# A condition around a loop that may have no turns, with its semaphores reset in stages

## The chip, the cores and the metric

The kernel runs on one core of a Trainium2 chip. Times are device microseconds of that core. The engines are named as the profile names them: PE (matrix multiply; PEld its weight loads), DVE (vector), ACT (scalar), POOL (GpSimd) and SP (SyncE, which here issues DMAs). Each engine has a sequencer of its own (PEq, DVEq and so on in the rows), which runs branches, register moves, semaphore waits and drains; the profile does not count these as busy.

## The reference

Three parts run one after the other on 1152 tokens: attention with rotary positions, a dense feed-forward layer, and a layer of eight experts, of which each token goes to one. Cut to what matters here:

```python
def _moe2_ref(x, w_gate, w1, w2, capacity):
    expert_idx = np.argmax(x @ w_gate, axis=1)
    ...
    for i in range(N):                      # tokens in order, up to capacity for each expert
        e = expert_idx[i]
        if counts[e] < capacity:
            disp[e, counts[e]] = x[i]
            ...
    h = np.maximum(np.einsum('ecd,edf->ecf', disp, w1), 0.0)
    y = np.einsum('ecf,efd->ecd', h, w2)
    ... # out[i] = gate_w[i] * y[expert_idx[i], pos[i]] for kept tokens
```

How many tokens an expert gets is known only at run time.

## The kernel before, in words

`whole` builds the attention (`Attention.run`, an order written out by hand) and then `Experts.run`. The last runs the dense layer in three column ranges (`first`), and between them sorts the tokens of each of the two batches by expert (`route`). Sorted tokens are cut into items: an item is up to 288 tokens of one expert. Four items always exist, of fixed widths (`STATIC`), and are written out in straight code: three calls of `second` and one of `few`. An input that spreads its tokens more evenly makes more items than four, up to 20. For these the kernel holds a loop, `tc.For_i(4, n, 1)` at line 1214, whose body gathers an item's rows, turns them, runs one expert and sends the result. `route` writes the number of items into the last place of the table `etab`, and line 1213 loads it into a register of every engine as `n`.

The last piece of straight work is `few`. Its last step is on POOL: `send` (line 1081), a DMA that scatters 96 rows to `out`. Behind it on POOL stand the load of `n`, the loop's entry, and the end of the program.

A layer under the kernel records the operations, orders them and puts in the semaphores. Each engine counts its work on a semaphore of its own; DMAs that SP issues count on eight semaphores (DMAHW0 to DMAHW7), and DMAs that POOL issues on eight others (DMASW0 to DMASW7). After the loop, the numbers on these semaphores must be the same whether or not it had a turn. So an engine that skips the loop adds to its semaphores what the loop would have added. For the POOL DMAs one instruction on POOL does it: INC_SWDGE_SEM in the profile, ISA in the listings below.

The built program of before has these blocks in this order behind the straight code: *skip* (taken when `n` is 4), *reset* (a barrier and the reset of all semaphores, before each further turn), *body*, *exit*, *end*. In *skip* POOL waits until all of its DMAs, the last `send` among them, have landed, and then adds. In *exit* each of the five engines passes a list of twelve waits on pairs of semaphores: all DMAs, all engines. In *end* SP waits for nothing more; every engine drains, meets the others in a barrier that POOL leads, POOL clears the semaphores, and there is a second barrier.

A drain is the instruction by which the program has an engine finish what it has in hand. The rows give the end block line 1244, the loop and its blocks line 1214.

Of the kernel before, what the change touches and what calls it, by code (L numbers as in the profile page):

```python
# [322 lines left out]
class Attention:  # L323
# [280 lines left out]
    def run(self, spare):  # L604
        for _, _, f, args in plan(len(spare)):
            self.pin((lambda: spare[args[0]]()) if f == "spare" else (lambda: getattr(self, f)(*args)))
# [57 lines left out]
class Experts:  # L664
# [527 lines left out]
    def run(self):  # L1192
        nc, tc = self.nc, self.tc
        sp = [mybir.EngineType.SP]
        found, x = {}, {}

        def turn(i):
            x[i] = self.turn(found[i][1], i)

        self.logits = [self.two.tile([TT, NT, E], F32, name=f"logits{b}", bufs=1) for b in range(B)]  # L1200
        for n, (k0, k1) in enumerate(zip(CUTS, CUTS[1:])):
            self.first(k0, k1, {0: (10, self.setup), len(CUTS) - 2: (0, lambda: turn(0))}.get(n))
            if n == 0:
                self.clear()
            for b in range(B):
                if k0 < (b + 1) * NT <= k1:
                    self.route(b, self.logits[b])
                    for k in range(2 * b, 2 * b + 2):
                        found[k] = self.gather(k, [b], *STATIC[k])
        for i in range(3):  # L1210
            self.second(found[i][0], x[i], self.expert(i, sp), ((4, 0, 4)[i], lambda: turn(i + 1)))
        self.few(found[3][0], x[3], self.expert(3, sp))
        n = nc.values_load(self.etab[0:1, ITEMS:ITEMS + 1], min_val=4, max_val=ITEMS)
        with tc.For_i(4, n, 1) as i:
            ent, rows = self.gather(i, [0, 1])
            self.cut = []
            self.second(ent, self.turn(rows, 0), self.expert(i, sp))
# [30 lines left out]
```

## Time and profile before

| | us |
|---|---|
| median of 3 runs | 460.74 (460.49 to 464.29) |
| the profiled execution, its own time | 461.19 |
| its span, from first to last instruction | 459.4 |
| the rest, around the span | 1.8 |

The span counts every instruction, those of the sequencers too. PE is busy for 436.6 us of it (95%), at a mean granted clock of 0.994. What lies in the last microseconds is not matrix work, and is read from the rows of the sequencers, line by line in narrow stretches.

### The profile page before, as it was taken

To read this page: it belongs to the slowest core of one execution; us is meant where nothing else is said; L and a number is where in the kernel's file an instruction comes from. 1 tells how busy PE (TensorE), PEld (TensorE's weight loads), DVE (VectorE), ACT (ScalarE), POOL (GpSimd) and SP (SyncE) were. 2 spreads that over 40 slices of the span, in tenths; PEclk is the share of its full clock that TensorE was granted. 3 is DMA by queue.
4 is the path that set the end of the run, shared out by engine and by line. 5 is a ranking of instruction groups with operands and counts; after the bars stand their busy time and mean duration, and the time that the engine had idled before them with its cause. 6 is when DMAs were issued, how large, how long until landed. Compare 5 with 4: busy or idle time off the path is not lost.

```text
span 459.4 us, 9065 instructions
## 1 busy us (share of the span) xinstructions
PE 436.6 (95%) x3380; PEld 373.4 (81%) x3380; DVE 309.7 (67%) x693; ACT 266.0 (58%) x558; POOL 123.9 (27%) x130
## 2 busy tenths in 40 slices
PE   7899999999988999999999999999999999999991
PEld 3556666666565878788999999999999999999980
DVE  5866866677968889997355344457846697765670
ACT  1788888888858252445453445475566455464560
POOL 1589877983210000000000000000526033701020
PEclk9999999999999999999999999999999999999997
DMA  8614421331315756550011600001175446874510
GB/s 279 235 71 145 144 72 75 144 122 30 139 53 177 257 165 245 216 188 1 0 36 34 224 0 1 0 27 46 6 271 182 145 139 186 247 260 157 185 51 16
DMA packets 20319, 57.11 MB, mean 124 GB/s; under 512 B 3749, under 2 KB 5957, under 8 KB 20272
## 3 DMA queue, kind: packets, MB, share of 16 engines
q1 hardware_dynamic: 17584, 52.09, 33.4%
q0 software_dynamic: 1728, 3.62, 2.6%
q10 hardware_dynamic: 960, 0.79, 0.5%
q8 instruction: 28, 0.46, 0.4%
q14 instruction: 19, 0.16, 0.1%
HBM read 49.91 MB, written 6.66 MB: 123 GB/s over the span
## 4 chain that ended last, share of the span: by engine, by line
PE 57%; issue 15%; DVE 10%; DMA 9%; POOL 4%; ACT 3%; SPq 0%; POOLq 0%; DVEq 0%; ACTq 0%
PE h L758 18%; PE y L784 17%; PE t L576 7%; PE s L461 6%; PE t L501 5%; DMA slots<-entry,r_at 2%; DMA raw<-in_w_in 2%; DVE pp L473 2%; POOL slots L959 2%; PE tr L849 2%; POOL out L1081 2%; DVE wf L659 2%; PE s L450 2%; DMA ent<-slots 1%; DVE m L658 1%
## 5 line engine op out<-in xcount | busy, mean ns | idle before, releaser
L758 PE MATMUL h<-xt,hl 128*128 128x288 f32 (+3 forms) x864 | 159.9, 324 | 3.5 <-ACT hl L744 1.4
L758 PEld LDWEIGHTS h<-xt,hl 128*128 128x128 f32 x864 | 135.2, 188 | 11.2 <-ACT hl L744 2.4
L784 PE MATMUL y<-gh,hl 128*128 128x288 f32 (+3 forms) x576 | 123.9, 322 | 0.4 <-ACT gh L794 0.4
L745 DVE TENSOR_TENSOR hl<-wf,hl 128x1024 fp32r<-128x1024 f32 x72 | 87.9, 1224 | 51.3 <-ACT hl L744 51.2
L744 ACT ACTIVATE hl<-wf 128x1024 fp32r<-128x1024 f32 x72 | 76.1, 1059 | 49.6 <-DVE wf L659 26.1
L784 PEld LDWEIGHTS y<-gh,hl 128*128 128x128 f32 x576 | 94.9, 188 | 4.3 <-ACT gh L794 0.8
L784 PE MATMUL y<-gl,hl 128*128 128x288 f32 (+3 forms) x288 | 77.0, 321 | 0.0
L959 POOL DMA_INDIRECT slots<-entry,r_at x12 | 15.0, 1254 | 208.0 <-ACT hl L744 184.3
L793 ACT ACTIVATE g<-h 128x480 f32<-128x480 f32 (+2 forms) x48 | 23.2, 491 | 63.1 <-PE h L758 54.3
L473 DVE TENSOR_SCALAR_CACHE_REDUCE pp<-s 128x576 f32<-128x576 f32 x64 | 45.8, 754 | 16.2 <-PE s L461 15.8
L485 ACT ACTIVATE pp<-pp,nm 128x576 f32<-128x576 f32 x64 | 49.3, 771 | 12.5 <-DVE pp L473 11.8
L784 PEld LDWEIGHTS y<-gl,hl 128*128 128x128 f32 x288 | 50.9, 188 | 1.8
L795 DVE TENSOR_TENSOR gl<-g,gh 128x480 fp32r<-128x480 f32 (+2 forms) x48 | 26.5, 555 | 27.5 <-ACT gh L794 27.2
L434 POOL TENSOR_TENSOR qk<-qk,turns 128x640 f32<-128x640 f32 (+1 forms) x28 | 41.5, 1507 | 9.5 <-DMA qk<-in_qk 9.5
L461 PE MATMUL s<-qk 64*128 64x288 f32 x256 | 40.8, 421 | 3.1 <-DVE pp L473 1.4
L382 ACT ACTIVATE pt<-t 128x512 f32<-128x512 f32 (+1 forms) x65 | 32.8, 538 | 10.4 <-PE t L501 10.3
L576 PE MATMUL t<-pt,vr 128*64 128x288 f32 x256 | 38.3, 419 | 0.1
L501 PEld LDWEIGHTS t<-ident,pp 64*128 64x128 f32 x576 | 23.7, 138 | 16.2 <-issue 4.2
L501 PE MATMUL t<-ident,pp 64*128 64x64 f32 x576 | 28.8, 230 | 2.6 <-ACT pt L382 0.9
L461 PEld LDWEIGHTS s<-qk 64*128 64x128 f32 x256 | 24.0, 188 | 8.3 <-DVE pp L473 2.6
L576 PEld LDWEIGHTS t<-pt,vr 128*64 128x64 f32 x256 | 15.5, 136 | 13.4 <-issue 3.8
L794 ACT ACTIVATE gh<-g 128x480 fp32r<-128x480 f32 (+2 forms) x48 | 24.8, 525 | 1.1
(173 smaller groups left out, 473.6 us busy)
## 6 DMA issues: line engine op xcount, KB each, us to landing
wf<-in_w SPq DMA_DIRECT2D x32, 512.0 KB, 4.5
qk<-in_qk SPq DMA_DIRECT2D x14, 640.0 KB, 5.5
raw<-in_w_in SPq DMA_DIRECT2D x16, 512.0 KB, 4.4
raw<-in_w_out SPq DMA_DIRECT2D x16, 512.0 KB, 3.8
vr<-in_v SPq DMA_DIRECT2D x8, 320.0 KB, 5.0
x<-row SPq DMA_DIRECT2D x12, 192.0 KB, 2.1
out<-zero SPq DMA_DIRECT2D x9, 256.0 KB, 3.0
qk<-in_qk SPq DMA_DIRECT2D x1, 384.0 KB, 4.8
```

Of the source, the lines that this page charges most:

```text
L382: return e.activation(out=out, in_=x, func=AF.Copy)
L434: e.tensor_tensor(out=u, in0=u, in1=self.turns[:, k, ts], op=ALU.mult)
L461: nc.tensor.matmul(both[h][:, n, 0:HALF], q[hs, at:at + P], k[hs, key:key + HALF], start=True, stop=True)
L473: self.nc.vector.tensor_scalar(out=self.room(p, i).rearrange("p (n k) -> p n k", n=2), in0=self.open.pop(("s", p, i))[:, :, 0:HALF], scala ...
L485: self.nc.scalar.activation(out=x, in_=x, func=AF.Exp, scale=-1.0, bias=self.nm[p % 2][:, i:i + 1], accum_out=self.sum[p % 2][:, i:i + 1],)
L501: self.nc.tensor.transpose(banks[b][:, at:at + 64], x[bs], self.ident[bs, bs])
L576: self.nc.tensor.matmul(o[h * 64:h * 64 + 64], x, y, start=j < 2, stop=j > 7)
L744: nc.scalar.activation(out=hl[:, 0], in_=t, func=AF.Copy)
L745: self.last = nc.vector.tensor_tensor(out=hl[:, 1], in0=t, in1=hl[:, 0].bitcast(F32), op=ALU.subtract).ins
L758: self.nc.tensor.matmul(h, u, v, start=m == 0, stop=m == len(ops) - 1)
L784: nc.tensor.matmul(y[j][:, 0:w], u, v, start=f == LAG and m == 0, stop=f == n + LAG - 1 and m == 2)
L795: nc.vector.tensor_tensor(out=gl, in0=g, in1=gh.bitcast(F32), op=ALU.subtract)
```

## The change

One line. The loop stands inside a condition, and its semaphores are reset in stages.

```diff
         self.few(found[3][0], x[3], self.expert(3, sp))
         n = nc.values_load(self.etab[0:1, ITEMS:ITEMS + 1], min_val=4, max_val=ITEMS)
-        with tc.For_i(4, n, 1) as i:
+        with tc.If(n > 4, label="more"), tc.For_i(4, n, 1, iteration_sync="staggered") as i:
             ent, rows = self.gather(i, [0, 1])
             self.cut = []
             self.second(ent, self.turn(rows, 0), self.expert(i, sp))
```

Staged reset: the body is cut into four stages. Work in them counts on semaphores of the loop's own, and an engine that enters a stage resets those of the next, behind a wait that all engines have left the stage before the last. The block *reset* with its barrier is gone; the body grows, on PE from 222 instructions of the built program to 234, on POOL from 31 to 40, on SP from 32 to 48.

The condition: the built program now has, behind the straight code, *true arm* (adds, a barrier, the loop's entry), the loop's *skip*, *body*, *exit* and *after* (a second barrier), *false arm*, *end*. With `n` at 4 an engine branches from the straight code to the false arm, which lies behind all of the others (on POOL behind 51 instructions; the branch from *skip* to *exit* in the program before goes over 39, *reset* and *body*), and from there goes on to *end*, which lies next to it. Up to line 1213 every engine has the same instructions in the same order as before; six of the last PE instructions there count up their semaphore in one step instead of four.

On POOL, from the load of `n` on (the straight code's end, then what was *skip*; ISA is INC_SWDGE_SEM, and a row names the semaphores waited for since the row ahead of it):

```order
 L1213 TENSOR_LOAD etab [waits DMAHW2_49,DMAHW1_49,DMAHW3_49,DMAHW0_49,DMAHW4_49,DVE_49,DMAHW5_49,PE_49,DMAHW6_49,Activation_49,Pool_49]
 L1214 COMPARE_AND_BRANCH
-L1214 ISA [waits DMASW4_49,DMASW5_49,DMASW3_49,DMASW6_49,DMASW2_49,DMASW7_49,DMASW1_49,DMASW0_49]
+L1214 ISA [waits barrier_Pool_Activation_PE_DVE_SP_gather,DMASW4_49,DMASW3_49,DMASW2_49]
+L1214 COMPARE_AND_BRANCH
 L1214 UNCONDITIONAL_BRANCH
```

The block that skips the loop, with its wait for all eight semaphores, is gone from here; the rows with a plus are the true arm, which is not taken when `n` is 4.

On POOL, behind the loop's body (the first branch is the loop's own, then come *exit*, and with a plus *after* and the false arm; the last row is the clear in *end*):

```order
 L1214 REGISTER_ALU
 L1214 COMPARE_AND_BRANCH
-L1214 UNCONDITIONAL_BRANCH [waits DMASW5_49,DMASW4_49,DMASW6_49,DMASW3_49,DMASW7_49,DMASW2_49,DMAHW0_49,DMASW1_49,DMAHW1_49,DMASW0_49,DMAHW2_49,SP_sequencer_49,DMAHW3_49,DVE_sequencer_49,DMAHW4_49,PE_sequencer_49,DMAHW5_49,Activation_seque
+L1214 UNCONDITIONAL_BRANCH [waits sem_stage_2_6336]
+L1214 UNCONDITIONAL_BRANCH [waits barrier_Pool_Activation_PE_DVE_SP_gather]
+L1214 ISA [waits DMASW4_49,DMASW3_49,DMASW2_49]
+L1214 UNCONDITIONAL_BRANCH
 L1244 ISA [waits barrier_Pool_Activation_PE_DVE_SP_gather]
```

The list of twelve waits in *exit* is gone from POOL, and in the same way from PE, DVE and ACT. The false arm's INC_SWDGE_SEM waits for three of the eight semaphores, at counts that the last `send` (it counts on DMASW1) does not belong to. It adds to as many semaphores as before. A list of all waits, the last `send` among them, now stands on SP alone, at the head of *end* (twelve instructions and a drain; the listing names no waits of drains).

## Rows read from the trace of the kernel before

**Rows 1.** Stretches of the span: length, busy us of each engine (instructions), clock, DMA.

```profile
core 0: us, PE busy (x) PEld busy (x) DVE busy (x) ACT busy (x) POOL busy (x), PEclk, DMA share, GB/s
0.00:440.00 440.00, 427.52 (x3327) 366.60 (x3328) 302.70 (x681) 262.16 (x548) 120.20 (x126) 1.00 0.38 128
440.00:452.00 12.00, 9.11 (x55) 6.77 (x53) 7.00 (x13) 3.88 (x10) 3.67 (x4) 1.00 0.18 51
452.00:460.00 8.00, 0.00 (x0) 0.00 (x0) 0.00 (x0) 0.00 (x0) 0.00 (x0) 0.61 0.08 20
```

**Rows 2.** Lines 959, 1036, 1031: POOL's DMAs; ns min/median/max, first and last start us.

```profile
L959 POOL DMA_INDIRECT slots<-entry,r_at x12: 915/1130/1980, 325.5 to 381.0; - x12
L1036 POOL DMA_INDIRECT got<-x,ent x9: 964/1237/1812, 344.7 to 395.0; - x9
L1031 POOL DMA_DIRECT2D ent<-slots x4: 567/713/737, 341.5 to 386.4; - x4
```

**Rows 3.** The tile `out` from 440 us on: the sends, and issue to landing.

```profile
L1081 POOL DMA_INDIRECT out<-row,ent x4: 915/918/920, 441.7 to 450.6; - x4
...
DMA to landing us min/median/max: 2.7/2.8/2.8
```

**Rows 4.** POOL's sequencer at lines 1213 and 1214, narrow stretches in order of time.

```profile
L1213 POOLq TENSOR_LOAD <-etab x1: 496/496/496, 450.8 to 450.8; - x1
L1214 POOLq COMPARE_BRANCH  x1: 54/54/54, 451.4 to 451.4; - x1
L1214 POOLq EVENT_SEMAPHORE  x3: 17/43/43, 451.5 to 451.7; - x3
L1214 POOLq EVENT_SEMAPHORE  x1: 1683/1683/1683, 451.8 to 451.8; - x1
L1214 POOLq INC_SWDGE_SEM  x1: 866/866/866, 453.5 to 453.5; - x1
L1214 POOLq COMPARE_BRANCH  x1: 38/38/38, 454.4 to 454.4; - x1
L1214 POOLq EVENT_SEMAPHORE  x12: 42/43/43, 454.6 to 455.5; - x12
L1214 POOLq COMPARE_BRANCH  x1: 38/38/38, 455.6 to 455.6; - x1
```

**Rows 5.** Line 1244 from 455 us on: the drains and barriers of the end block.

```profile
L1244 POOLq DRAIN  x1: 2835/2835/2835, 455.8 to 455.8; - x1
L1244 PEldq DRAIN  x1: 8/8/8, 455.9 to 455.9; - x1
L1244 POOLq EVENT_SEMAPHORE  x4: 17/17/17, 458.6 to 459.3; - x4
L1244 POOLq DRAIN  x2: 40/69/98, 458.8 to 459.1; - x2
```

**Rows 6.** Line 1238, the start of the program: POOL's drain and INC_SWDGE_SEM there.

```profile
L1238 POOLq INC_SWDGE_SEM  x1: 27/27/27, 0.1 to 0.1; - x1
L1238 POOLq DRAIN  x1: 183/183/183, 0.4 to 0.4; - x1
```

**Rows 7.** Line 1214 on the other engines: branches of PE, ACT, DVE, waits of SP.

```profile
L1214 PEldq COMPARE_BRANCH  x3: 97/193/3473, 449.6 to 455.7; - x3
L1214 PEldq COMPARE_BRANCH  x1: 3473/3473/3473, 449.9 to 449.9; - x1
L1214 ACTq COMPARE_BRANCH  x2: 38/46/53, 447.8 to 448.0; - x2
L1214 DVEq COMPARE_BRANCH  x2: 51/54/56, 451.1 to 451.3; - x2
L1214 SPq COMPARE_BRANCH  x1: 58/58/58, 427.8 to 427.8; - x1
L1214 SPq EVENT_SEMAPHORE  x12: 27/28/28, 454.3 to 455.0; - x12
```

**Rows 8.** Queues of instruction fetches: 449.8 to 453.4 us, then 455.7 to 458.65 us.

```profile
q8 instruction: 1, 0.02, 2.0%
...
q14 instruction: 1, 0.01, 1.2%
```

## The prediction

> **What bounds the kernel now.** I read the stretches of the span first [rows 1]. Up to 440 us PE is busy for 427.5 of 440 us; up to 452 us for 9.1 of 12. From 452 us to the end no engine does counted work, and the span still goes on to 459.4 us. The change leaves every instruction ahead of line 1214 where it was, so only the stretch from the load of `n` on can move, about 8 of 459.4 us. One thing has to be settled before: does the loop run on this input? POOL's gathers say no [rows 2]: nine at line 1036 are the 3, 2, 3 and 1 blocks of the four fixed items, the last starts at 395.0 us, and a turn of the loop would add six late ones. So `n` is 4, no turn is taken, and the staged reset works on nothing. What is left is how an engine gets past the loop.
>
> In the last 8 us I follow POOL, since its work ends last: the last send starts at 450.6 us [rows 3], PE's branch is at 449.6 us and ACT's at 447.8 us [rows 7]. POOL's sequencer, step by step [rows 4, 5]:
>
> - load of `n` at 450.8 us, 0.50 us; branch at 451.4 us;
> - *skip*: four waits from 451.5 us, the last of 1.68 us, to 453.5 us. It ends with the landing of the last send: 450.6 us and 2.8 us from issue to landing [rows 3] make 453.4 us;
> - INC_SWDGE_SEM 0.87 us, to 454.4 us; the other engines' lists begin there, SP's at 454.3 us [rows 7], so they all waited for it;
> - *exit*: twelve waits, 454.6 to 455.6 us; branch; drain begins at 455.8 us;
> - drain of 2.84 us, to 458.6 us. The other engines' drains are done (PE's took 8 ns, at 455.9 us), so POOL's sets the end;
> - barrier, clear, barrier: 458.6 to 459.4 us, 0.8 us.
>
> **What the change removes.** POOL's wait for the send, 453.5 − 451.6 = 1.9 us (one wait of about 0.1 us stays, on semaphores that were complete long before). POOL's list in *exit*: from the end of INC_SWDGE_SEM at 454.4 us to the drain at 455.8 us are 1.4 us, of which branch and step to the drain, 0.2 us, stay: 1.2 us. Together 3.1 us. Counted the other way: from the first wait at 451.5 us to the drain POOL took 4.3 us, and will take 0.1 + 0.87 + 0.2 = 1.2 us.
>
> **What it keeps, and the price of each.** INC_SWDGE_SEM goes over the same eight semaphores; at the start of the program, with no DMA behind it, one took 0.03 us [rows 6], here 0.87 us [rows 4]. I take 0.87 us, since the same DMAs are behind it; the lower end would save 0.8 us more.
>
> The drain is the term that decides. It took 2.84 us although POOL's last DMA had landed 2.4 us before it began, so it did not wait for a transfer. At the start, with four fills and no DMA behind it, a drain took 0.18 us [rows 6]; the two after the long one took 0.04 and 0.10 us [rows 5]. So the length goes with what POOL did before. POOL issued 34 DMAs (12, 9 and 4 [rows 2], nine sends of which four are in [rows 3]), 83 ns for each if it goes through them: an estimate. These 34 are the same after. I take 2.84 us from wherever it starts; the ends are 0.1 us (gone) and 5.2 us (it ends that long after the landing, whenever it starts).
>
> New on the path is the jump to the false arm. POOL's jump from *skip* over 39 instructions to *exit* cost 0.2 us between the branch at 454.4 us and the next wait [rows 4]; the new one goes over 51. I take it at that, within the steps above. The other end is PE's: 3.47 us [rows 7].
>
> **Sum.** Arm at 451.5 us, INC_SWDGE_SEM 451.6 to 452.5, drain 452.7 to 455.5, end 456.3 us: 3.1 us less than 459.4. The profiled execution would take 461.19 − 3.1 = 458.1 us, and the median, 0.45 us below it, 460.74 − 3.1 = **457.6 us**.
>
> **What covers the rest.** SP now holds the only list, and the last send's landing is in it. It passes that at 453.4 us, and the ten steps behind it at (455.0 − 454.3) / 11 = 0.06 us each, to 454.0 us: 1.5 us ahead of POOL's drain. Nobody else waits for SP's list; nothing is queued behind it but SP's own drain. If the drain cost nothing, the list would set the end, at 454.0 + 0.1 + 0.8 = 454.9 us, and the gain would be 4.5 us. PE jumps over the body again, from 449.6 us, stalls 3.5 us and is done near 453.4 us, 2.1 us ahead of the drain's end. A second stall there, on the way from the arm to *end*, would end at 456.9 us and cost 1.4 us of the gain, but *end* lies next to the arm. ACT and DVE come past the arm by 448.3 and 451.6 us.
>
> **Rivals.**
>
> *The drain is short.* If the 2.84 us are not the drain's own, the send's landing and SP's list set the end: 460.74 − 4.5 = 456.2 us. For it: one packet of instructions is fetched in the stretch of the drain [rows 8], as one is in the stretch of PE's stall; code that is fetched only then, after POOL entered the last block, may be what held it, and another layout need not have it there. Against: a stall stands in the row of PE's branch, and POOL's branch ahead of the drain took 38 ns.
> The Trainium skill (VectorE: DVE Perf Modes, The DRAIN you can't avoid) says that the drains at a program's start and end take about 12 ns on all engines. By that page the time would be this rival's; the drains of PE agree with it (8 ns), POOL's long one does not [rows 5].
>
> *The drain is bound to INC_SWDGE_SEM.* From that instruction's start at 453.5 us to the drain's end at 458.6 us are 5.1 us. If it hands work on that the drain waits for, only its own move counts, 1.9 us: 458.8 us. For it: nothing else ran on POOL. Against: POOL's sequencer took the twelve waits at an even 0.09 us behind it.
>
> *The drain is bound to the send.* It ends 5.2 us after the landing, which does not move: 460.7 us. For it: only a drain behind DMAs was long. Against: all DMAs had landed.
>
> *Slower: POOL stalls at the jump.* The false arm lies behind the whole body, and PE's jump over the body cost 3.47 us with a fetch in that stretch [rows 7, 8]. If POOL's jump at 451.4 us costs the same, with no other work to cover it, the 3.1 us become −0.4: 461.1 us. It decides from a stall of 3.1 us on, and a second one, at *end*, would make 464.6 us. For it: POOL has more to jump over than before. Against: 39 instructions cost it nothing, 51 are little more, and PE's body has over 200.
> The Trainium skill (Runtime: NRT & Kernel Launch, Instruction fetch mechanics) has a rule for it: a taken branch whose target is outside the two pages at hand stalls for a fetch, with 256 instructions to a page. By that rule POOL's 51 are likely inside, and PE's row agrees with a stall for a longer way.
>
> *The change doesn't do what it says* in this way: without a turn the staged reset has nothing to do. That is part of the forecast, not a rival with a time.
>
> **How the numbers follow.** Forecast 457.6 us, 0.56. Short drain 456.2 us, 0.11. Bound to INC_SWDGE_SEM (or a second stall on PE, 459.0 us) 458.8 us, 0.11. Bound to the send 460.7 us, 0.09. Stall on POOL 461.1 us or more, 0.10. Anything else 0.03. The range takes in the cases from 456.2 to 460.7 us and the 0.25 us by which two of the three runs before differ: 455.9 to 461.0 us; it leaves out most of the stall and the rest, 0.13. By over 1% (below 456.1 or above 465.3 us, about what a measurement of this kernel can tell from no change): faster is half of the short drain and a little scatter, 0.08; slower a double stall and scatter, 0.04; within 1%, 0.88. That it is faster by less than 1% is by far the likeliest.
>
> **What would show it.** In the profile after, lines 1213 and before should stand at the same times to 0.1 us. POOL's INC_SWDGE_SEM should start at 451.6 us with no long wait ahead of it; its drain at 452.7 us with 2.8 us; SP's twelve waits should end near 454.0 us; the span 456.3 us. A long COMPARE_BRANCH on POOL would show the stall; a drain of 0.1 us the short one; a drain of 4 us that it is bound to INC_SWDGE_SEM, of 5.9 us that it is bound to the send. I am wrong if POOL's drain does not keep its length, or if something ahead of line 1214 moves.

## The result and the profile after

| | before | after |
|---|---|---|
| median of 9 runs each | 460.8 us (459.56 to 464.29) | 457.5 us (456.65 to 458.86) |
| ratio to before | | 0.9919, 95% interval 0.9895 to 0.9944 |
| profiled execution, own time | 461.19 us | 457.5 us |
| its span | 459.4 us | 455.8 us |
| from the start of the last send to the end of the span | 459.4 − 450.6 = 8.8 us | 455.8 − 450.2 = 5.6 us |

The changed kernel is 3.3 us faster by the medians, 3.7 us by the ratio, 3.6 us by the two spans. Of the last, the stretch from the last send on gives 3.2 us; the other 0.4 us lie ahead of it, where the change has nothing. That is scatter: the changed kernel was run again beside later experiments, and there its last send started at 451.0 us and its span ended at 456.6 us, again 5.6 us later. So below, every kernel is read from the start of its last send on.

The stretches of the span after, to be laid beside [rows 1]:

```profile
core 0: us, PE busy (x) PEld busy (x) DVE busy (x) ACT busy (x) POOL busy (x), PEclk, DMA share, GB/s
0.00:440.00 440.00, 428.06 (x3331) 366.95 (x3332) 303.38 (x681) 262.04 (x548) 120.61 (x126) 1.00 0.38 128
440.00:452.00 12.00, 8.72 (x52) 6.39 (x49) 6.60 (x13) 3.88 (x10) 3.67 (x4) 1.00 0.20 58
452.00:460.00 8.00, 0.00 (x0) 0.00 (x0) 0.00 (x0) 0.00 (x0) 0.00 (x0) 0.78 0.03 10
```

The work is the same; what became shorter is the part of the last row in which nothing counted happens, up to 455.8 us instead of 459.4 us.

POOL after: first the sends (the tile `out` from 440 us on, for [rows 3]), then its sequencer in order of time, lines 1213, 1214 and 1244 in narrow stretches (for [rows 4, 5]):

```profile
L1081 POOL DMA_INDIRECT out<-row,ent x4: 913/918/920, 441.3 to 450.2; - x4
...
DMA to landing us min/median/max: 2.7/2.7/2.7
```

```profile
L1213 POOLq TENSOR_LOAD <-etab x1: 504/504/504, 450.4 to 450.4; - x1
L1214 POOLq COMPARE_BRANCH  x1: 50/50/50, 451.0 to 451.0; - x1
L1214 POOLq EVENT_SEMAPHORE  x1: 43/43/43, 451.2 to 451.2; - x1
L1214 POOLq INC_SWDGE_SEM  x1: 882/882/882, 451.3 to 451.3; - x1
L1244 POOLq DRAIN  x1: 2835/2835/2835, 452.2 to 452.2; - x1
L1244 POOLq EVENT_SEMAPHORE  x4: 17/17/17, 455.1 to 455.7; - x4
```

Where [rows 4] had four waits, the last of 1683 ns, there is one of 43 ns; the twelve waits behind INC_SWDGE_SEM are gone, and the drain stands right behind it. INC_SWDGE_SEM and the drain kept their lengths, the drain to the nanosecond: 2835 ns. POOL is past it at 455.0 us, and the end takes 0.8 us as before.

The other engines on lines 1214 and 1244, for [rows 5, 7]:

```profile
L1214 ACTq COMPARE_BRANCH  x1: 54/54/54, 447.3 to 447.3; - x1
L1214 PEldq COMPARE_BRANCH  x1: 3338/3338/3338, 449.1 to 449.1; - x1
L1214 DVEq COMPARE_BRANCH  x1: 72/72/72, 450.7 to 450.7; - x1
L1244 SPq EVENT_SEMAPHORE  x1: 692/692/692, 452.2 to 452.2; - x1
L1244 PEldq DRAIN  x1: 8/8/8, 452.7 to 452.7; - x1
L1244 SPq DRAIN  x1: 13/13/13, 453.5 to 453.5; - x1
```

SP now waits for the landing of the last send (692 ns, to 452.9 us) and is through its list at 453.5 us; PE stalls 3.3 us at its branch and is through at 452.7 us. POOL's drain, to 455.0 us, covers both.

### The profile page after: what moved, and what is told of

Its sections match the earlier page's. It is cut to its first block, busy times and chain, and to the rows that moved or that the text cites. A ratio compares the mean times of both kernels' runs of the same rounds, so it can differ in the third digit from the quotient of the medians.

```text
span 455.8 us, 8990 instructions
## 1 busy us (share of the span) xinstructions
PE 436.8 (96%) x3380; PEld 373.3 (82%) x3380; DVE 310.0 (68%) x693; ACT 265.9 (58%) x558; POOL 124.3 (27%) x130
## 4 chain that ended last, share of the span: by engine, by line
PE 63%; issue 13%; DVE 9%; DMA 7%; ACT 3%; POOL 3%; SPq 0%; POOLq 0%; DVEq 0%; ACTq 0%
PE h L758 20%; PE y L784 19%; PE t L576 8%; PE s L461 6%; PE t L501 5%; DVE pp L473 2%; PE tr L849 2%; POOL out L1081 2%; DMA raw<-in_w_out 2%; PE s L450 2%; DMA raw<-in_w_in 2%; DMA slots<-entry,r_at 1%; DVE m L658 1%; DVE wf L659 1%; DMA turns<-in_turns 1%
```

## The experiments

All from the profiled execution, times in us; "tail" is the time from the start of the last send to the end of the span, taken before rounding. "Early drain" is one more drain on POOL in an idle stretch, explained further down.

| kernel | last send | INC_SWDGE_SEM | POOL's drain at the end | span | tail | median |
|---|---|---|---|---|---|---|
| before | 450.6 | 0.87 | 2.84 | 459.4 | 8.8 | 460.8 |
| after | 450.2 | 0.88 | 2.84 | 455.8 | 5.6 | 457.5 |
| condition alone | 449.7 | 0.87 | 2.84 | 457.0 | 7.3 | 459.7 |
| staging alone | 450.8 | 0.89 | 2.84 | 460.1 | 9.3 | 461.4 |
| no loop | 449.6 | none | see below | 454.6 | 4.9 | 457.6 |
| after, early drain | 450.6 | 0.21 | 1.49 | 454.8 | 4.2 | 456.0 |
| after, 17 more DMAs | 450.8 | 1.22 | 4.23 | 458.1 | 7.3 | 459.8 (1 run) |
| before, drain with one DMA behind it | 449.7 | 0.19 | 0.14 | 455.1 | 5.4 | 456.9 |
| before, drain with six DMAs behind it | 450.4 | 0.31 | 0.54 | 456.3 | 5.9 | 457.9 (1 run) |

**The two halves of the change.** First the condition without the staging:

```diff
-        with tc.If(n > 4, label="more"), tc.For_i(4, n, 1, iteration_sync="staggered") as i:
+        with tc.If(n > 4, label="more"), tc.For_i(4, n, 1) as i:
```

> The condition alone: the loop inside it resets its semaphores as before. Theory (the gain is two waits, one for each half of the change): POOL's wait for the last send stands in the false arm again, so the 1.9 us for it are lost, and POOL's list of twelve waits is still gone, 1.2 us. From the start of the last send to the end of the span: 2.8 us to its landing, 0.9 us INC_SWDGE_SEM, 0.2 us step, 2.84 us drain, 0.8 us for the end, 7.5 us, where the kernel before took 8.8 us and the changed one 5.6 us. Median 459.5 us, 1.2 us below before. Rival (the condition does all of it, by where the code then lies): 457.5 us. Rival (the staging does all of it): 460.8 us.

Measured: 459.71 us (458.52 to 461.22, 12 runs), ratio to before 0.9971, interval 0.9949 to 0.9992. POOL's sequencer in it, lines 1214 and 1244 in narrow stretches:

```profile
L1214 POOLq EVENT_SEMAPHORE  x1: 1537/1537/1537, 450.9 to 450.9; - x1
L1214 POOLq INC_SWDGE_SEM  x1: 866/866/866, 452.4 to 452.4; - x1
L1244 POOLq DRAIN  x1: 2835/2835/2835, 453.3 to 453.3; - x1
```

The wait for the send is back, the list of twelve waits is not. The tail is 7.3 us, 1.5 us below before and 1.7 us above after; the theory had 7.5 us. Neither rival holds: the condition takes away the list, and the wait for the send, which it leaves, goes only when the staging is added.

Then the staging without the condition:

```diff
-        with tc.If(n > 4, label="more"), tc.For_i(4, n, 1, iteration_sync="staggered") as i:
+        with tc.For_i(4, n, 1, iteration_sync="staggered") as i:
```

> The staged reset alone, without the condition: what the staging sets up, with a barrier of all engines, then runs ahead of the loop's branch, and a second barrier stands behind the loop. Theory: the send is not waited for and POOL has no list, but PE's stall at the jump over the body (3.3 to 3.5 us) now lies between the two barriers, where POOL waits for it. From the start of the last send: first barrier at 0.9 us, PE's stall to 4.5 us, drain to 7.3 us, end at 8.1 us, so 2.5 us above the changed kernel: 460.0 us, close to before. Rival (PE's stall is not met, or is over before the barrier): INC_SWDGE_SEM sets the second barrier at 2.3 us, end at 6.0 us: 457.9 us.

Measured: 461.43 us (460.33 to 465.12, 12 runs), ratio 1.0009, interval 0.9988 to 1.0031. PE's weight-load queue at line 1214 (from 452.1 us), then POOL's sequencer at lines 1214 and 1244 in order of time:

```profile
L1214 PEldq COMPARE_BRANCH  x1: 3642/3642/3642, 452.1 to 452.1; - x1
```

```profile
L1214 POOLq INC_SWDGE_SEM  x1: 887/887/887, 451.9 to 451.9; - x1
L1214 POOLq COMPARE_BRANCH  x3: 38/38/54, 452.9 to 453.1; - x3
L1214 POOLq EVENT_SEMAPHORE  x1: 17/17/17, 456.3 to 456.3; - x1
L1244 POOLq DRAIN  x1: 2835/2835/2835, 456.5 to 456.5; - x1
```

POOL waits for no landing in it (INC_SWDGE_SEM begins at 451.9 us, the send lands 2.8 us after 450.8 us) and has no list, but a barrier on either side of the branches. It is through its branches at 453.2 us and stands at the second barrier until 456.3 us: PE, held at the first barrier until 451.7 us, only then starts its stall of 3.6 us. The theory's mechanism held. Its size was short, 8.1 us against 9.3 us: PE reached the branch 0.4 us behind the barrier, the stall was 0.2 us longer than in the kernel before, and PE has 0.5 us of steps between it and the second barrier. So the staging alone brings no gain on this input, since it puts PE's stall in the way of POOL; the condition lets all engines go around both barriers.

**What bounds the tail without a loop.** The load of `n` and the loop are deleted:

```diff
-        n = nc.values_load(self.etab[0:1, ITEMS:ITEMS + 1], min_val=4, max_val=ITEMS)
-        with tc.If(n > 4, label="more"), tc.For_i(4, n, 1, iteration_sync="staggered") as i:
...
-            self.second(ent, self.turn(rows, 0), self.expert(i, sp))
```

> The load of n and the repeated body are left out (the code for surplus items, of which this input has none). What stays is the last send, POOL's drain and SP's list. Theory (the drain's 2.84 us are its own and begin as soon as POOL has issued its last send): from the start of the send 0.95 us, drain to 3.8 us, end at 4.6 us, 1.0 us below the changed kernel: 456.5 us; SP's list ends at 3.4 us, 0.4 us ahead. Rival (the drain waits until the send has landed and then takes its 2.84 us): end at 6.4 us, 458.3 us. Rival (the drain's length comes from INC_SWDGE_SEM or from the blocks that are jumped over): a drain of 0.1 us, SP's list sets the end at 4.3 us, 456.2 us.

Measured: 457.64 us (456.35 to 461.35, 12 runs), ratio 0.9937, interval 0.991 to 0.9963. POOL's drain and SP's list in the end block (line 1240 there; the first row's 7411 ns is SP's wait for the landing):

```profile
L1240 SPq EVENT_SEMAPHORE  x6: 17/28/7411, 444.9 to 453.9; - x6
L1240 POOLq DRAIN  x2: 102/2240/4377, 449.4 to 454.0; - x2
L1240 SPq DRAIN  x2: 7/10/13, 452.6 to 452.7; - x2
```

The drain is queued ahead of the send's start and ends at 449.4 + 4.4 = 453.8 us; SP is through at 452.7 us. So without INC_SWDGE_SEM and without any block to jump over the drain is still long and sets the end: the rival that it comes from those falls. So does the rival that it takes all of its 2.84 us behind the landing: that came at 452.3 us, 1.4 us before the drain's end. The tail is 4.9 us, 0.7 us below after, not 1.0 us: from the end of the send's work on POOL, at 449.6 + 0.9 = 450.5 us, the drain took 3.2 us, not 2.84 us (the reason follows below, with the landings). The median did not go below that of after; the runs spread over 5 us, and the two intervals overlap. The whole time can't tell 0.7 us here; the tail can.

**What the drain's length goes with.** One more drain on POOL, in a stretch where it has nothing to do, ahead of the last send:

```diff
+        with tc.issue_after(self.sent[-1].ins):
+            nc.gpsimd.drain()
         self.few(found[3][0], x[3], self.expert(3, sp))
```

In the changed kernel:

> The changed kernel with one more drain on POOL, ahead of the last of its 34 DMAs, where POOL has nothing to do for 5 us. Theory (a drain goes through the DMAs that POOL issued since the drain before): the early one takes 2.8 us beside PE's work, the last one 0.1 to 0.3 us; SP's list then sets the end at 4.3 us from the start of the last send, 1.3 us below the changed kernel: 456.2 us. Rival (a drain behind software DMAs costs 2.84 us each time): both drains 2.84 us, the time unchanged, 457.5 us. Rival (it was a stall of the code in the last block, not of the drain): early drain 0.1 us, last one 2.84 us, 457.5 us.

And in the kernel before, where nothing of POOL's is still under way when its last drain begins:

> The kernel before, unchanged but for one more drain on POOL ahead of the last of its 34 DMAs. There POOL waits for the send's landing ahead of INC_SWDGE_SEM and the drain, so that neither holds any landing. Theory (both go through the DMAs since the drain before, here one): INC_SWDGE_SEM 0.2 us, the last drain 0.1 to 0.2 us, 3.3 us below the kernel before: 457.5 us, as much as the change itself brought. Rival (the drain costs 2.84 us behind any DMA): 460.2 us from INC_SWDGE_SEM alone.

The same in the kernel before, but with the drain behind the first item's last send:

> The kernel before with one more drain on POOL behind the first item's last send: 28 DMAs ahead of it, six behind it. Theory (a price for each DMA): the last drain 0.1 + 6 x 83 ns, 0.6 us, INC_SWDGE_SEM 0.2 + 5 x 20 ns, 0.3 us. Rival (a price that is reached at once): 2.84 us and 0.88 us. Rival (all is cheap until a queue is full): 0.1 to 0.2 us.

And the changed kernel with more DMAs:

```diff
                 self.clear()
+                spare = self.one.tile([1, 17, 4], I32, name="spare")
+                for k in range(17):
+                    nc.gpsimd.dma_start(out=spare[:, k], in_=self.x2[0][0:1, 0:4].bitcast(I32))
```

> The changed kernel with 17 more DMAs of 16 bytes each on POOL, early in the program (they read a piece of memory into a tile that nobody uses): 51 DMAs instead of 34. Theory (INC_SWDGE_SEM and the drain go through POOL's DMAs, one by one): the drain grows by 17 x 83 ns to 4.2 us, INC_SWDGE_SEM by 17 x 20 ns (0.88 us behind 34, 0.21 us behind one) to 1.2 us, the end comes 1.7 us later. Rival (they go through the rows that the DMAs moved, some 96 for each of the others, one for each of these): both unchanged, 0.88 and 2.84 us. Rival (a fixed price for whatever came before): both unchanged.

POOL's sequencer at the end, in narrow stretches; first the kernel before with one DMA behind the early drain, then with six, then the changed kernel with 51 DMAs (the lines are moved by what was added):

```profile
L1216 POOLq INC_SWDGE_SEM  x1: 194/194/194, 452.5 to 452.5; - x1
L1246 POOLq DRAIN  x1: 135/135/135, 454.1 to 454.1; - x1
```

```profile
L1217 POOLq INC_SWDGE_SEM  x1: 306/306/306, 453.2 to 453.2; - x1
L1247 POOLq DRAIN  x1: 537/537/537, 454.9 to 454.9; - x1
```

```profile
L1217 POOLq INC_SWDGE_SEM  x1: 1221/1221/1221, 451.8 to 451.8; - x1
L1247 POOLq DRAIN  x1: 4227/4227/4227, 453.1 to 453.1; - x1
```

With 1, 6, 34 and 51 DMAs since the drain before, the drain took 135, 537, 2835 and 4227 ns: 80, 82 and 82 ns for each further DMA. INC_SWDGE_SEM took 194, 306, 866 (882 in the changed kernel) and 1221 ns: 22, 20 and 20 ns for each. DMAs of 16 bytes cost as much as DMAs of whole tiles, so it is not the rows moved; a fixed price and a full queue fall too. The kernel before with the early drain was timed: 456.9 us (456.5 to 457.26, 4 runs), ratio 0.992, interval 0.989 to 0.995. One drain in an idle stretch brought as much as the change.

In the changed kernel with the early drain, POOL's sequencer in narrow stretches and SP's wait for the landing:

```profile
L1213 POOLq DRAIN  x1: 4821/4821/4821, 443.4 to 443.4; - x1
L1216 POOLq INC_SWDGE_SEM  x1: 211/211/211, 451.6 to 451.6; - x1
L1246 POOLq DRAIN  x1: 1492/1492/1492, 451.9 to 451.9; - x1
```

```profile
L1246 SPq EVENT_SEMAPHORE  x1: 1368/1368/1368, 451.9 to 451.9; - x1
```

The early drain is over at 448.2 us, ahead of the last send at 450.6 us. It took 4.8 us, not the expected 2.8 us: at 443.4 us two of the 33 DMAs ahead of it were not through on POOL yet, and from the end of the second, at 445.0 us, it took 3.2 us, as the drain in the kernel without a loop did. The last one was not 0.1 to 0.3 us: it ends at 453.4 us, where SP sees the landing at 453.3 us. With one DMA behind it, still in flight, the drain lasts until that has landed; where it had landed before, it took 0.14 us. For the time this changes nothing, since SP's list ends later, at 454.0 us. Measured: 456.03 us (454.94 to 456.63, 6 runs), ratio 0.9878, interval 0.9849 to 0.9908.

The landings account for the drains that took longer than 82 ns for each DMA. These drains had begun before the last DMA ahead of them landed (times to 0.01 us from the trace's records):

| drain | DMAs since the drain before | last of them lands | drain ends | between |
|---|---|---|---|---|
| after, early drain: the one at the end | 1 | 453.28 | 453.37 | 0.09 |
| before, drain with six DMAs behind it: the early one | 28 | 404.61 | 405.81 | 1.20 |
| after, early drain: the early one | 33 | 446.85 | 448.25 | 1.40 |
| no loop: the one at the end | 34 | 452.32 | 453.76 | 1.44 |

The second of them, begun long ahead of the landing, with the last send ahead of it:

```profile
L1214 POOLq DRAIN  x1: 11552/11552/11552, 394.3 to 394.3; - x1
```

```profile
L1081 POOL DMA_INDIRECT out<-row,ent x1: 922/922/922, 399.3 to 399.3; - x1
...
DMA to landing us min/median/max: 5.3/5.3/5.3
```

With one DMA the drain ends 0.09 us behind the last landing, and each further DMA adds 41 ns, half of the 82 ns, however early the drain began. So half of its price seems to be work that begins only once all have landed. In the changed kernel the landing came 0.7 us into the drain, when the first half of its 2.84 us was not over, and it cost nothing. That the price has two halves is read from these lengths alone; no run was made for it.

**After and early drain side by side.** Both kernels once more on one chip:

> The changed kernel once more, beside the next run on the same chip: 457.5 us, INC_SWDGE_SEM 0.88 us, drain 2.84 us, 5.6 us from the start of the last send to the end of the span.

> The changed kernel with the early drain on POOL once more. Theory (a drain goes through the DMAs since the drain before, 82 ns each, and is not over before they have landed): INC_SWDGE_SEM 0.2 us, the last drain ends with the landing, SP's list sets the end, 4.2 us from the start of the last send, 1.4 us below the changed kernel: 456.1 us. Rival (the 456.0 us measured before came from the stretch ahead of the last send): the same as the changed kernel.

Measured: after 457.76 us (456.82 to 458.71, 6 runs), ratio 0.9917, interval 0.9889 to 0.9945; with the early drain 456.42 us (455.04 to 459.37, 6 runs), ratio 0.9897, interval 0.9863 to 0.9931. The tails are 456.6 − 451.0 = 5.6 us and 455.6 − 451.4 = 4.2 us, INC_SWDGE_SEM 882 and 211 ns, the drain 2835 and 1492 ns, all as the first time. The medians are 1.3 us apart, and the tails 1.4 us; the two intervals overlap, so the whole times alone don't settle it. On an input with surplus items neither was timed.

## Why the prediction was right, point by point

- **No turn of the loop; only what lies behind the load of `n` moves.** Right. That all ahead of it would stand within 0.1 us was too tight: the last send came 0.4 us earlier, by scatter (in the kernels here it starts anywhere from 449.6 to 451.4 us). That the median lies within 0.1 us of the forecast is in part luck: the nine runs spread over 2.2 us.
- **POOL's two waits, 1.9 + 1.2 us.** Right in sum, 3.1 us against 3.2 us in the tail. The split was off: by the tails, the condition alone brings 1.5 us (the list) and the staging the other 1.7 us (the wait). Two errors of the sum offset each other. Behind INC_SWDGE_SEM I left 0.2 us for branch and step to the drain; the drain began 0.03 us behind it (451.3 + 0.88 to 452.2 us). Ahead of INC_SWDGE_SEM I counted 0.2 us from the branch on (451.4 to 451.6 us), which leaves out most of the jump; branch, jump and one wait took 0.3 us (451.0 to 451.3 us).
- **INC_SWDGE_SEM 0.87 us, drain 2.84 us.** Right: 882 and 2835 ns. So was the reason. The 83 ns for each of POOL's DMAs, only divided from one row in the prediction, are 82 ns by the runs with 1, 6 and 51 DMAs.
- **The jump to the false arm at 0.2 us.** Right: branch at 451.0, wait at 451.2 us.
- **The cover.** SP's list was done 1.5 us ahead of the drain's end (453.5 and 455.0 us), as forecast; PE 2.3 us ahead, forecast 2.1 us. No stall of PE's followed on the way to *end*: its drain stands at 452.7 us, behind one stall of 3.3 us.
- **The short drain.** Falls: the drain kept its length, and it goes with the DMAs, not with a fetch of code. In the kernel without a loop no packet of instructions was fetched while the drain ran, and it was no shorter. (PE's stall had two such packets in its stretch, not one: the view of [rows 8] also has one on q14.) The Trainium skill (VectorE: DVE Perf Modes, The DRAIN you can't avoid) has about 12 ns for the drains at a program's start and end; PE's 8 ns fit that, POOL's do not: 2835 ns here, and 40 ns for its shortest, with no DMA to go through.
- **The drain bound to INC_SWDGE_SEM or to the send.** Both fall: from INC_SWDGE_SEM's start to the drain's end are 3.7 us now, not 5.1 us, and without INC_SWDGE_SEM the drain was no shorter; and in the changed kernel it began 0.7 us ahead of the landing and still took 2835 ns. What is true of the second: about half of the drain's price comes behind the last landing, which shows only where the first half is over by then.
- **POOL stalls at the jump.** Falls: 50 ns for the branch. The price that it feared exists, though. PE's stall of 3.6 us came onto the path in the staging alone, where a barrier stands on either side of it, and ate the whole gain.

## What to carry to other kernels

A wait at the end of a program is worth what stands behind it on the same engine: here the send's landing was waited for in front of 3.7 us of POOL's own work, and moved beside it. If an engine issues many DMAs from software, look at the length of its drain and divide it by their number; a drain in an idle stretch earlier takes that work off the end. And staging that frees a loop of one barrier can place two others around a branch: look which engine stalls between them.

## What the runs showed of the hardware

- POOL's drain takes 82 ns for each DMA that POOL issued since its last drain, whatever the DMA moved, and INC_SWDGE_SEM 20 ns for each; an earlier drain shortens both (34 to 1: from 2835 to 135 ns and from 866 to 194 ns).
- A drain that begins well before the last landing ends behind it by 0.09, 1.20, 1.40 and 1.44 us for 1, 28, 33 and 34 DMAs, 41 ns for each further one. That is why the drain queued right behind the send took 3.2 us in the kernel without a loop, 0.4 us more than the 2.84 us.
- POOL passed all its branches in 38 to 54 ns, PE's over the body took 3.3 to 3.8 us each time. The Trainium skill (Runtime: NRT & Kernel Launch, Instruction fetch mechanics) lets a branch stall when its target lies outside the two pages at hand. POOL's short branches agree with it; whether PE's target lay outside, no trace shows, and no run varied the distance of PE's jump.
